# ScalarE's moves and exponentials in a hardware loop over heads, with one set of sum columns, in a one-core decode attention kernel

## The chip, the cores and the metric

The kernel runs on one core of a Trainium2 chip. The metric is the device time of one execution in microseconds (us).

## The reference

```python
# q: (1, 32, 1, 128), k and v: (1, 8, 65536, 128), all bf16
k = jnp.repeat(k, 4, axis=1)          # four query heads share one key/value head
v = jnp.repeat(v, 4, axis=1)
scores = jnp.einsum("bhqd,bhkd->bhqk", q, k) * 128 ** -0.5
p = _softmax(scores, axis=-1)
return jnp.einsum("bhqk,bhkd->bhqd", p, v)
```

One new token attends to 65,536 keys. Each byte of K and V (268.4 MB) is read once and used for four query rows.

## The kernel before

Each of the eight heads is two blocks of 32,768 keys, so there are sixteen blocks. For a block, VectorE transposes K, PE multiplies it with the queries (scores), ScalarE moves the scores from PSUM (where PE writes them) to SBUF (where VectorE and ScalarE then read them), VectorE and GpSimd find the maximum, ScalarE takes exponentials and their sums, and PE multiplies the result with V ("PV"). SyncEngine issues the loads, and sixteen DMA engines carry them out. K has two buffers, V has one. PE's code was in a hardware loop already (its instructions stand in the program once, and a branch goes back to them); ScalarE's and VectorE's were written out for all sixteen blocks.

ScalarE, before (this is what the change folds):

```python
        def move(j, u):
            if u == 0 and j >= 1:
                ac.wait_ge(ex_s, R * j)
            ac.wait_ge(qk_s, (j * U + u + 1) * GU)
            # ... cut: views fr (PSUM) and to (SBUF)
            for x in range(A):
                for a in range(A):
                    ins = ac.activation(to[...], fr[...], AF.Copy)      # 16 per call
            ins.then_inc(mv_s, 1)

        def exponent(i):
            h, b = divmod(i, C)
            ac.wait_ge(hma_s, i + 1)
            ac.activation(negb[b], ..., AF.Copy, scale=-scale).then_inc(nb_s, 1)
            if b:
                ac.wait_ge(df_s, h + 1)
                ac.activation(wgt, dif, AF.Exp, scale=scale).then_inc(wg_s, 1)
            # ... cut: waits for nb_s, mv_s
            if i >= 1:
                ac.wait_ge(pv_s, 2 * i)
            for g_ in range(R):
                ac.activation(pv[:, g_, :], sv[:, g_, :], AF.Exp, ...,
                              accum_out=rsum[h % 2][b][:, g_:g_ + 1]).then_inc(ex_s, 1)

        for j in range(N):              # N = 16, unrolled
            for u in range(U):          # U = 4
                move(j, u)
            exponent(j)
```

VectorE's end of a block, before. `weigh` rescales the first block of a head once the second one's maximum is known:

```python
        def collect(i):
            h, b = divmod(i, C)
            dv.wait_ge(pv_s, (i + 1) * 2)      # PV of block i is done
            if b == 0:
                dv.tensor_copy(o1, acc[:, 0:R]).then_inc(co_s, 1)
                return
            weigh(h)                           # three small operations
            # ... cut: add, wait for the sums' all-reduce (ls_s), reciprocal, multiply
```

The loads, whose order fixes what each DMA engine does: K of block j, then V of block j-1, each 8.4 MB as 128 rows. The last blocks are cut into pieces.

```python
        def load_k(i):
            if i >= NK:
                sp.wait_ge(tr_s, (i - NK + 1) * G)      # block i-2 is transposed
            # ... cut: the loads
        def load_v(i):
            if i < N - HALVED:
                if i >= 1:
                    sp.wait_ge(pv_s, 2 * i)             # PV of block i-1 is done
                # ... cut: the load, and the last blocks in pieces
```

## Time and profile before

| | before |
|---|---|
| device time, first three runs | 635.66 us median (635.41 to 635.75) |
| span of the profiled execution | 634.3 us |
| mean data rate over the span | 424 GB/s |
| busiest compute engine | VectorE, 54% |
| 8 KB instruction fetches in the span | 14 |

The page of the kernel before. The first lines are the busy time of each engine with its share of the span and its number of instructions, then the busy tenths of the DMA engines in forty slices, then the DMA queues with packets, MB, and share of sixteen engines' time:

```profile
span 634.3 us, 18751 instructions
...
PE 269.9 (43%) x8194; PEld 243.9 (38%) x8194; DVE 341.1 (54%) x411; ACT 275.7 (43%) x1178; POOL 10.5 (2%) x32
...
DMA  9999999999999999999999999999999999999995
...
DMA packets 6824, 268.68 MB, mean 424 GB/s; under 512 B 1045, under 2 KB 1045, under 8 KB 1685
...
q1 hardware_dynamic: 6612, 268.45, 98.4%
q8 instruction: 5, 0.08, 0.1%
q14 instruction: 15, 0.11, 0.0%
```

Data fill the DMA engines almost from the first slice to the last, and no compute engine passes 54%. So the kernel is limited by how fast the engines move 268 MB. The lines for q8 and q14, the queues of the instruction fetches (packets that the page labels "instruction"; e3 and e6 show that an engine's added code brings more of them), look like nothing: 0.19 MB of instructions, 0.1% of the time of sixteen engines. The share is an average over sixteen engines. If a fetch delays only one of them, 0.1% of sixteen is 1.6% of one. And at the end of this kernel a load was complete only with its slowest engine: in the tail below, PE's product at 629.67 us had still waited for V, though fifteen of the sixteen engines had moved all their data by 627.67 us.

The longest waits that matter here (engine, line, what it waited for: us in total, times, longest):

```profile
DVE ktb L276 <- DMA kbuf<-in_k_dram: 158.4, 17, 12.0
...
ACT pts L383 <- PE acc L196: 34.9, 15, 8.8
POOL small L154 <- DVE small L309: 30.8, 8, 12.2
...
DVE small L305 <- PE acc L196: 18.2, 7, 2.7
...
DVE small L322 <- POOL small L154: 3.4, 7, 0.5
```

VectorE waits for K from memory. ScalarE's exponentials wait for PV; the bias and weight that they need are ready earlier. This is the timeline of ScalarE near the end of block 7 (start us, duration us, engine, line, operation, idle before it):

```profile
302.61 0.21 ACT L372 ACTIVATE small<-small 128x4 f32<-128x4 f32 x1 [1.37 <-POOL small L162]
...
302.81 0.20 ACT L375 ACTIVATE small<-small 128x4 f32<-128x4 f32 x1
304.65 0.33 SPq L115 DMA_DIRECT2D vbuf<-in_v_dram  x1
...
304.74 0.86 ACT L383 ACTIVATE pts<-scs,small 128x256 bf16<-128x256 f32 x1 [1.73 <-PE acc L196]
```

Bias and weight are finished at 303.01 us, PV releases the exponentials at 304.74. ScalarE has about 1.7 us of slack there.

The tail of the timeline, PE's last PV products and the output store:

```profile
626.09 1.85 PE L196 MATMUL acc<-pts,vbuf 128*128 128x4 bf16 x64 [1.46 <-DMA vbuf<-in_v_dram]
...
628.47 1.01 PE L196 MATMUL acc<-pts,vbuf 128*128 128x4 bf16 x32 [0.54 <-DMA vbuf<-in_v_dram]
...
629.67 0.59 PE L196 MATMUL acc<-pts,vbuf 128*128 128x4 bf16 x16 [0.19 <-DMA vbuf<-in_v_dram]
...
630.77 0.57 PE L196 MATMUL acc<-pts,vbuf 128*128 128x4 bf16 x16
...
631.88 0.68 SPq L147 DMA_DIRECT2D out_dram<-oTX  x1
```

The first three of these groups of products each wait for a piece of V.

**Packets, engine by engine.** The page does not show single DMA engines, but the trace keeps start, duration, size and queue of every packet. Between 100 and 600 us sixteen packets are under way in 494 of the 500 us, and each starts within about 10 ns of the end of another. So packets can be chained by abutting times into sixteen chains, which I take for the sixteen engines. Two chains that end at the same nanosecond can swap names; the sorted times below hardly depend on that. From the kernel before, the start of the first 16 KB packet on each chain (the last K block) and the end of the last value packet:

```
                        earliest   9th     15th    16th (last)   us from the span's start
start of last K block    563.91   564.92  567.42   570.34
end of the data          626.17   626.82  627.67   630.46
```

One engine, called the straggler from here on, is about 2.9 us behind all others. The fetches on queue 14, 8 KB each, start at 34.5, 75.7, 95.6, 171.3, 222.7, 243.6, 291.1, 366.8, 425.6, 428.4, 489.1, 562.4, 597.8 and 618.8 us (the page counts 15 packets because of one 40-byte packet at the start). This is what one of them does to the data on its engine:

```
start us   took ns   bytes    queue
361.993     2422     65536    data
364.412     2422     65536    data
366.831      309      8192    q14 instruction
367.136     2798     65536    data
369.931     2419     65536    data
```

The next packet starts 0.302 us late and itself takes 0.376 us longer than the usual 2.422, so the engine loses 0.68 us to a fetch of 0.31 us. The data packets behind the nine ScalarE fetches from 34.5 to 562.4 us take 2.789 to 2.801 us. Followed through the chains, the nine ScalarE fetches from 34.5 to 562.4 us lie on the straggler: nine times 0.68 is 6.1 of the 6.4 us by which it starts the last K block after the earliest engine. VectorE's four fetches (75.7, 243.6, 428.4 and 597.8 us) cost more: the 64 KB packets after the first three take 3.080 us each, so the loss at 243.6 us is 0.97 us.

### The profile page before, as it was taken

Reading aid. Unit: us, or ns where it says so; the run is one execution under the profiler, and the core shown is the slowest. Engines: PE = TensorE matmul, PEld = TensorE weight load, DVE = VectorE, ACT = ScalarE, POOL = GpSimd, SP = SyncE. Lnnn points to the kernel's source line nnn. Section 1 sums busy time; section 2 is a strip of 40 time slices with the busy share of each in tenths; the row PEclk is TensorE's granted clock in tenths of the full one; section 3 lists DMA queues with packets and bytes.
Section 4 is the critical chain, followed back from the end, with each engine's and each line's share of the span. In section 5 each row is a group of like instructions: output and inputs, shape, how many; then the busy total and the mean of one; then the engine's idle time right before and its main releaser. Section 6 shows DMA issues by size and latency. Waiting matters only on the chain.

```text
span 634.3 us, 18751 instructions
## 1 busy us (share of the span) xinstructions
PE 269.9 (43%) x8194; PEld 243.9 (38%) x8194; DVE 341.1 (54%) x411; ACT 275.7 (43%) x1178; POOL 10.5 (2%) x32
## 2 busy tenths in 40 slices
PE   1314536144361534526255261553614437146525
PEld 1214436144361433525245261442614436146424
DVE  4649166390853809447193571926619176295710
ACT  0456425164351734617255261542616425165720
POOL 0000000000000000000000000000000000000000
DMA  9999999999999999999999999999999999999995
GB/s 365 433 446 426 434 426 439 438 422 446 422 442 434 430 426 434 446 413 451 422 446 426 434 430 430 446 414 455 413 450 422 438 426 438 438 401 437 431 349 222
DMA packets 6824, 268.68 MB, mean 424 GB/s; under 512 B 1045, under 2 KB 1045, under 8 KB 1685
## 3 DMA queue, kind: packets, MB, share of 16 engines
q1 hardware_dynamic: 6612, 268.45, 98.4%
q8 instruction: 5, 0.08, 0.1%
q14 instruction: 15, 0.11, 0.0%
q10 hardware_dynamic: 192, 0.03, 0.0%
HBM read 268.47 MB, written 0.01 MB: 423 GB/s over the span
## 4 chain that ended last, share of the span: by engine, by line
DMA 48%; DVE 27%; PE 14%; another core or an unknown queue 9%; SPq 1%; issue 1%; POOL 0%; DVEq 0%
DMA kbuf<-in_k_dram 30%; DVE ktb L276 25%; DMA vbuf<-in_v_dram 17%; PE acc L196 13%; PE qkb L185 1%; DVE small L283 1%; SPq L115 1%; POOL small L154 0%; PE acc L244 0%; DVE small L322 0%; DVE small L309 0%; DVE small L305 0%; DVE oTX L348 0%; DVE oTX L346 0%
## 5 line engine op out<-in xcount | busy, mean ns | idle before, releaser
L276 DVE STREAM_TRANSPOSE ktb<-kbuf 128x1024 int32<-128x1024 int32 x256 | 295.9, 1215 | 161.3 <-DMA kbuf<-in_k_dram 158.4
L366 ACT ACTIVATE scs<-qkb 32x64 f32<-32x64 f32 x1024 | 220.4, 215 | 281.5 <-PE qkb L185 270.3
L185 PE MATMUL qkb<-qblk,ktb 128*128 x4096 | 157.0, 176 | 343.4 <-DVE ktb L276 330.5
L185 PEld LDWEIGHTS qkb<-qblk,ktb 128*128 128x128 bf16 x4096 | 132.6, 105 | 367.5 <-issue 199.5
L196 PE MATMUL acc<-pts,vbuf 128*128 128x4 bf16 x4096 | 112.5, 166 | 17.9 <-DMA vbuf<-in_v_dram 17.4
L196 PEld LDWEIGHTS acc<-pts,vbuf 128*128 128x128 bf16 x4096 | 111.1, 104 | 19.6 <-DMA vbuf<-in_v_dram 15.8
L283 DVE TENSOR_REDUCE small<-scs 128x4 f32<-128x256 f32 x64 | 37.9, 593 | 61.4 <-ACT scs L366 61.4
L383 ACT ACTIVATE pts<-scs,small 128x256 bf16<-128x256 f32 x64 | 48.9, 853 | 34.9 <-PE acc L196 34.9
L162 POOL PARTITION_ALL_REDUCE small<-small x16 | 5.9, 370 | 575.0 <-DVE small L294 575.0
L383 ACT ACTIVATION_READ_ACCUMULATOR pts<-scs,small 128x1 f32 x64 | 13.7, 214 | 0.0
L316 DVE COPY small<-acc 128x4 f32<-128x4 f32 x8 | 1.3, 162 | 22.3 <-PE acc L196 22.3
L372 ACT ACTIVATE small<-small 128x4 f32<-128x4 f32 x16 | 3.3, 205 | 21.7 <-POOL small L162 21.7
L305 DVE TENSOR_TENSOR small<-small 128x4 f32<-128x4 f32 x8 | 1.3, 163 | 18.3 <-PE acc L196 18.2
L346 DVE TENSOR_TENSOR oTX<-acc,small 128x4 bf16<-128x4 f32 x1 | 0.2, 163 | 13.7 <-PE acc L196 13.7
L154 POOL PARTITION_ALL_REDUCE small<-small x8 | 3.4, 430 | 30.8 <-DVE small L309 30.8
L299 DVE TENSOR_TENSOR small<-small 128x4 f32<-128x4 f32 x8 | 1.3, 163 | 4.0 <-POOL small L162 4.0
L294 DVE TENSOR_REDUCE small<-small 128x4 f32<-128x16 f32 (+1 forms) x16 | 2.9, 184 | 0.5
L322 DVE RECIPROCAL small<-small 128x4 f32<-128x4 f32 x7 | 1.2, 178 | 3.4 <-POOL small L154 3.4
L307 DVE TENSOR_TENSOR small<-small 128x4 f32<-128x4 f32 x8 | 1.3, 157 | 2.7 <-ACT pts L383 2.7
L356 ACT ACT_TABLE_LOAD x1 | 1.3, 1283 | 2.7 <-issue 2.7
L375 ACT ACTIVATE small<-small 128x4 f32<-128x4 f32 x8 | 1.6, 205 | 0.0
L309 DVE TENSOR_TENSOR small<-small 128x4 f32<-128x4 f32 x8 | 1.3, 163 | 0.3
(19 smaller groups left out, 7.2 us busy)
## 6 DMA issues: line engine op xcount, KB each, us to landing
vbuf<-in_v_dram SPq DMA_DIRECT2D x3, 4096.0 KB, 25.5
kbuf<-in_k_dram SPq DMA_DIRECT2D x5, 2048.0 KB, 40.6
kbuf<-in_k_dram SPq DMA_DIRECT2D x1, 4096.0 KB, 22.3
vbuf<-in_v_dram SPq DMA_DIRECT2D x1, 2048.0 KB, 12.5
kbuf<-in_k_dram SPq DMA_DIRECT2D x2, 512.0 KB, 4.7
kbuf<-in_k_dram SPq DMA_DIRECT2D x1, 1024.0 KB, 7.3
vbuf<-in_v_dram SPq DMA_DIRECT2D x1, 1024.0 KB, 14.6
vbuf<-in_v_dram SPq DMA_DIRECT2D x1, 512.0 KB, 15.3
```

The costliest lines, as they stand in the source:

```text
L115: sp.dma_start(buf[:, a * D:b * D], src(t, i)[:, a * D:b * D]).then_inc(s, 16)
L154: g.partition_all_reduce(lsum, rhead, P, bass.bass_isa.ReduceOp.add).then_inc(ls_s, 1)
L162: g.partition_all_reduce(mtot if b else mfirst, hmax[:, b * R:(b + 1) * R], P, bass.bass_isa.ReduceOp.max,).then_inc(hma_s, 1)
L185: ins = pe.matmul(qkb[g // GU][:, at:at + A * R], lhsT=kt[:, be // NE, be % NE, n * P:(n + 1) * P], rhs=qblk[:, bass.ds(qcols[be], A * R)] ...
L196: ins = pe.matmul(acc[:, 0:R], lhsT=vbuf[:, t * D:(t + 1) * D], rhs=pts[:, t * R:(t + 1) * R], start=t == 0, stop=t == T - 1,)
L276: dv.transpose(to.rearrange("p (b t j) -> p b t j", b=NB, t=TG), fr.rearrange("p (t b i) -> p b t i", b=NB, t=TG),).then_inc(tr_s, 1)
L283: dv.tensor_reduce(hp[j % C][:, u * R:(u + 1) * R], scs[:, u * W:(u + 1) * W].rearrange("p (n g) -> p g n", g=R), AX.X, ALU.max,).then_inc ...
L294: dv.tensor_reduce(hmax[:, b * R:(b + 1) * R], hp[b].rearrange("p (u g) -> p g u", g=R), AX.X, ALU.max,).then_inc(hm_s, 1)
L366: ins = ac.activation(to[a * S4:(a + 1) * S4, x, :, :], fr[x * S4:(x + 1) * S4, a, :, :], AF.Copy)
L372: ac.activation(negb[b], mtot if b else mfirst, AF.Copy, scale=-scale).then_inc(nb_s, 1)
L375: ac.activation(wgt, dif, AF.Exp, scale=scale).then_inc(wg_s, 1)
L383: ac.activation(pv[:, g_, :], sv[:, g_, :], AF.Exp, bias=negb[b][:, g_:g_ + 1], scale=scale, accum_out=rsum[h % 2][b][:, g_:g_ + 1],).then ...
```

## The change

Its intent: run ScalarE's moves and exponentials in a hardware loop with one turn per head, two blocks a turn. This loop's body names the same buffers in each turn, so the two alternating sets of sum columns become one; so that they are free in time, VectorE's weighting moves ahead of the wait for PV, and ScalarE waits for it (`rh_s`) before it overwrites the sums.

```diff
-    rsum = [[cols(R) for _ in range(C)] for _ in range(2)]
+    rsum = [cols(R) for _ in range(C)]
 ... (VectorE: rsum[h % 2][b] becomes rsum[b])
             if b == 0:
                 dv.tensor_copy(o1, acc[:, 0:R]).then_inc(co_s, 1)
                 return
-            weigh(h)
 ...
             block_maximum(j)
+            if j >= C and j % C == 0:
+                weigh(j // C - 1)
             if j >= 1:
                 collect(j - 1)
 ... (ScalarE)
-        for j in range(N):
-            for u in range(U):
-                move(j, u)
-            exponent(j)
+        with nc.Fori(0, H, 1, engines=bass.OrderedEngineSet([ac.engine]), head_slot={ac.engine: 0}) as h:
+            for b in range(C):
+                ac.wait_ge(ex_s, h * (C * R) + b * R)
+                for u in range(U):
+                    ac.wait_ge(qk_s, h * (C * G) + (b * U + u + 1) * GU)
+                    move(b, u)
+                ac.wait_ge(hma_s, h * C + (b + 1))
+                ac.activation(negb[b], mtot if b else mfirst, AF.Copy, scale=-scale).then_inc(nb_s, 1)
+                if b:
+                    ac.wait_ge(df_s, h + 1)
+                    ac.activation(wgt, dif, AF.Exp, scale=scale).then_inc(wg_s, 1)
+                else:
+                    ac.wait_ge(rh_s, h)
 ... (waits for nb_s, mv_s, pv_s and the four exponentials as before, with h in the sums)
```

## The prediction

> **What bounds the kernel now.** The data transfers. The page gives 268.68 MB at a mean of 424 GB/s in a 634.3 us span, and the data queue's packets take 98.4% of sixteen engines' time. No compute engine passes 54%. By the groups view ScalarE waits for PE's scores before moves (270.3 us) and for PV before exponentials (34.9 us). In the timeline its bias and weight are done at 303.0 us, PV at 304.6: 1.6 us of slack, then 14 us idle before the next moves.
>
> **The sixteen DMA engines do not finish together.** By the trace's packet records the last value packets end at 626.2 to 627.7 us on fifteen engines and at 630.46 on one, and the tail waits for that one. At the last K block (first 16 KB packets) one engine starts at 570.34 us, the next latest at 567.42, the earliest at 563.92: it is 2.9 us behind the second-worst, 6.4 behind the best, and never idle at the tail, where others pause 1 to 2.5 us.
>
> **Why that one.** Beside the data, the trace has instruction fetches: queue 8, five of 16 KB, all before 48 us (PE's loop); queue 14, fourteen of 8 KB from 34.5 us on. Ten of these, about 65 us apart, fit ScalarE's unrolled code (76 instructions a block, 128 a fetch); four, about 170 us apart, fit VectorE. Tracked by abutting packets, the ScalarE fetches fall mostly on one engine; each delays a 64 KB packet by 0.30 us and stretches it from 2.42 to 2.79: 0.67 us. Ten make 6.7 us, which fits the straggler.
>
> **What the change removes.** It folds about 1220 ScalarE instructions into a body of about 200 (152 for moves and exponentials, four small, waits, register work)[...]. The arithmetic and the bytes of K and V stay. The ten fetches should become one to three early ones, 5 us or more off the straggler. The second-worst engine then sets the end, so only 2.9 us of it count (2.3 to 3.6).
>
> **What it adds and moves.** Register arithmetic and a branch on ScalarE, [...]inside the 1.6 us slack and the 14 us idle. VectorE's three weighting operations (0.16 us each) move ahead of the wait for PV, so the sums' all-reduce (0.43 us) leaves the time after PV on odd blocks; but VectorE's next transposes wait some 11 us for K: nothing gained. The new wait for the sums is met before PV ends.
>
> **The risk.** [...]This trace's PE loop[...]: seventeen turns[...], no fetch on queue 8 after 48 us. If ScalarE's loop refetches two or three pages a turn, 16 to 24 fetches replace ten, and it is 4 to 9 us slower.
>
> **Predicted:** 633.0 us, range 631.0 to 636.2. Faster by over 2%: 1%; within 2%: 97%; slower by over 2%: 2%.
>
> **What would show it.** Right: queue 14's packets fall from 15 to about 6, the last value packets on all engines end within about 1.5 us, mean GB/s rises by about 2, VectorE's wait for the sums (3.4 us) vanishes. Wrong: queue 14 has 20 packets or more; or the fetches go and one engine still lags by 3 us (then PE's fetches or something else made the straggler); or ScalarE becomes the releaser of exponentials in place of PV.

No term of the sum is cut: 635.7 us less the 2.9 us of the straggler's lead that count is 632.8, recorded as 633.0. The 128 instructions a fetch fit the traces and runs: ScalarE's fetches in the kernel before are about 66 us apart and a block takes 38.7 us, so a fetch lasts 1.7 blocks of 76 instructions, about 130; later 1280 added GpSimd instructions brought ten fetches and 640 brought five (e6, e8). A page in the risk is what one fetch brings; two or three of them a turn were the assumption. What remains of the risk's argument is PE's loop: in the kernel before its five fetches on queue 8 start from 14.4 to 47.0 us, and none follows.

## The result, and the profile after

The kernel after took 632.74 us (median; 632.66 to 632.87, four runs), beside 635.70 us (635.41 to 636.16) for the kernel before. The ratio is 0.9953, with a 95% interval of 0.9936 to 0.997. A ratio here and below is the mean time of one kernel's fast runs over the mean of the other's of the same rounds, so it is not quite the ratio of the medians. The gain of 3.0 us is clear of the noise, and far below the 2% that would be called faster.

The page of the kernel after, the lines that answer to those of before:

```profile
span 630.9 us, 18889 instructions
...
PE 270.0 (43%) x8194; PEld 244.0 (39%) x8194; DVE 340.4 (54%) x411; ACT 275.6 (44%) x1178; POOL 10.4 (2%) x32
...
DMA  9999999999999999999999999999999999999995
...
DMA packets 6816, 268.62 MB, mean 426 GB/s; under 512 B 1044, under 2 KB 1044, under 8 KB 1684
...
q1 hardware_dynamic: 6612, 268.45, 98.8%
q8 instruction: 5, 0.08, 0.1%
...
q14 instruction: 7, 0.06, 0.0%
```

The engines do the same work: ScalarE has 1178 instructions in both, 275.7 and 275.6 us busy. What fell is queue 14: fifteen packets to seven, 0.11 to 0.06 MB. Three of the seven are ScalarE's (at 7.0, 11.5 and 62.5 us), the other four VectorE's. The rate is up from 424 to 426 GB/s.

The same waits (line numbers have shifted):

```profile
DVE ktb L276 <- DMA kbuf<-in_k_dram: 162.2, 17, 11.5
...
ACT pts L387 <- PE acc L196: 34.2, 15, 9.8
...
DVE small L319 <- PE acc L196: 15.5, 7, 2.2
POOL small L154 <- DVE small L309: 13.2, 1, 13.2
```

ScalarE's exponentials wait for PV as long as before. The weighting no longer stands behind PV: what follows PV on odd blocks is now the addition (L319), and the 3.4 us that VectorE waited for the sums' all-reduce are gone from the head-by-head work. VectorE then waits longer for K (158.4 to 162.2 us): the time that the change gave VectorE was only waited out.

ScalarE at the end of block 7:

```profile
302.63 0.21 ACT L375 ACTIVATE small<-small 128x4 f32<-128x4 f32 x1 [1.36 <-POOL small L162]
...
302.83 0.21 ACT L378 ACTIVATE small<-small 128x4 f32<-128x4 f32 x1
304.67 0.33 SPq L115 DMA_DIRECT2D vbuf<-in_v_dram  x1
...
304.68 0.86 ACT L387 ACTIVATE pts<-scs,small 128x256 bf16<-128x256 f32 x1 [1.64 <-PE acc L196]
```

Bias and weight end at 303.04 us, 0.03 us later than before, and PV still releases the exponentials. The loop's register work does not show on this path.

The tail:

```profile
622.56 1.84 PE L196 MATMUL acc<-pts,vbuf 128*128 128x4 bf16 x64 [1.44 <-DMA vbuf<-in_v_dram]
...
624.98 1.01 PE L196 MATMUL acc<-pts,vbuf 128*128 128x4 bf16 x32 [0.57 <-DMA vbuf<-in_v_dram]
...
626.19 0.59 PE L196 MATMUL acc<-pts,vbuf 128*128 128x4 bf16 x16 [0.20 <-DMA vbuf<-in_v_dram]
...
627.34 0.57 PE L196 MATMUL acc<-pts,vbuf 128*128 128x4 bf16 x16
...
628.45 0.67 SPq L147 DMA_DIRECT2D out_dram<-oTX  x1
```

The product over the last piece but two (the first group of 16) starts at 626.19 us, before at 629.67: 3.5 us earlier. That is more than the 3.0 us between the medians, because the profiled execution of the kernel before was a slow one for it (636.09 us against a median of 635.70). The engines, by the packet records:

```
                        earliest   9th     15th    16th (last)   us from the span's start
start of last K block    564.02   564.76  567.20   567.48
end of the data          623.67   624.23  626.21   627.04
```

The earliest nine engines reach the last K block when they did before. The engine that was alone at 570.34 us has gone; the last is now at 567.48, which is 2.86 us earlier and about where the second-worst stood.

### The profile page after: what moved, and what is told of

Its sections match the earlier page's. It is cut to its first block, busy times and chain, and to the rows that moved or that the text cites. A ratio compares the mean times of both kernels' runs of the same rounds, so it can differ in the third digit from the quotient of the medians.

```text
span 630.9 us, 18889 instructions
## 1 busy us (share of the span) xinstructions
PE 270.0 (43%) x8194; PEld 244.0 (39%) x8194; DVE 340.4 (54%) x411; ACT 275.6 (44%) x1178; POOL 10.4 (2%) x32
## 4 chain that ended last, share of the span: by engine, by line
DMA 66%; DVE 22%; PE 10%; SPq 1%; issue 1%; DVEq 0%
DMA kbuf<-in_k_dram 59%; DVE ktb L276 21%; PE acc L196 8%; DMA vbuf<-in_v_dram 7%; PE qkb L185 2%; DVE small L283 1%; SPq L115 1%; PE acc L244 0%; DVE oTX L349 0%; DVE oTX L347 0%; DVEq L346 0%
## 5 line engine op out<-in xcount | busy, mean ns | idle before, releaser
L276 DVE STREAM_TRANSPOSE ktb<-kbuf 128x1024 int32<-128x1024 int32 x256 | 295.9, 1212 | 165.1 <-DMA kbuf<-in_k_dram 162.2
L319 DVE TENSOR_TENSOR small<-acc,small 128x4 f32<-128x4 f32 x7 | 1.1, 162 | 15.5 <-PE acc L196 15.5
```

The source lines that it names most:

```text
L276: dv.transpose(to.rearrange("p (b t j) -> p b t j", b=NB, t=TG), fr.rearrange("p (t b i) -> p b t i", b=NB, t=TG),).then_inc(tr_s, 1)
```

## The experiments

Theory A: each of ScalarE's instruction fetches delays one DMA engine by about 0.67 us; ScalarE's written-out code put ten of them on one engine; a load waits for its slowest engine; the loop took seven of the ten away, and the end moved up to the next-worst engine. Rivals: B, the gain is the weighting that left VectorE's time after PV, or the single set of sums; C, fetches do no harm and something else held that engine back; D, the number of executed ScalarE instructions matters, not their fetching; E, only ScalarE's code matters because it is on the softmax path.

All outputs are right. "Fetches" are 8 KB packets on queue 14 in the span; VectorE's four are in each count unless noted.

| run | what it is | us, median (range) | before, same rounds | ratio (95%) | fetches |
|---|---|---|---|---|---|
| e1_unrolled | after, loop written out | 635.67 (635.45 to 636.20) | 635.89 | 0.9999 (0.9985 to 1.0013) | 14 |
| e2_pairs | before, loop over two heads | 632.83 (632.54 to 632.93) | 635.89 | 0.9953 (0.9939 to 0.9966) | 8 |
| e3_pad_unrolled | before, +1216 ScalarE instructions | 642.25 (642.13 to 642.26) | 635.89 | 1.01 (1.0085 to 1.0116) | 23 |
| e4_pad_loop | after, the same 1216 in the loop | 632.85 (632.78 to 632.89) | 635.89 | 0.9953 (0.994 to 0.9967) | 8 |
| e5_quads | before, loop over four heads | 638.80 (638.75 to 638.93) | 635.48 | 1.0052 (1.0038 to 1.0066) | 18 |
| e6_pad_pool | after, +1280 GpSimd instructions | 635.95 (635.59 to 636.04) | 635.48 | 1.0005 (0.9991 to 1.0018) | 17 |
| e7_dve_loop | after, VectorE looped too | 631.46 (631.36 to 632.03) | 635.48 | 0.9938 (0.9924 to 0.9951) | 6 |
| e8_pad_pool_half | after, +640 GpSimd instructions | 632.52 (632.50 to 632.75) | 635.61 | 0.9954 (0.994 to 0.9967) | 12 |
| e9_after_again | after | 632.86 (632.66 to 632.98) | 635.61 | 0.9958 (0.9944 to 0.9971) | 7 |
| e10_dve_loop_again | as e7 | 632.10 (631.62 to 632.34) | 635.61 | 0.9945 (0.9931 to 0.9958) | 6 |

### The two parts apart: e1 and e2

e1 keeps all of the change but the loop:

```diff
-        with nc.Fori(0, H, 1, ...) as h:
+        for h in range(H):
```

> The kernel after with ScalarE's hardware loop written out again; one set of sum columns, the new wait and the moved weighting stay. Theory A (instruction fetches delay one DMA engine): fourteen 8 KB fetches after 30 us come back, one engine lags the next by about 3 us again, 635.7 us (635.0 to 636.4). Rival B (the gain comes from the weighting leaving VectorE's time after PV, or from the single set of sums): 632.7 us.

Measured: 635.67 us, ratio 0.9999. The moved weighting, the new wait and the single set of sums are worth nothing. The last engine starts the last K block at 570.20 us, the next one at 567.43: the straggler is back, with the fetches (the page's line for queue 14):

```profile
q14 instruction: 14, 0.11, 0.0%
```

e2 is the other half: the kernel before with a loop over pairs of heads, so that the two sets of sums can stay and the weighting stays behind PV.

```diff
-        for j in range(N):
-            for u in range(U):
-                move(j, u)
-            exponent(j)
+        with nc.Fori(0, H // 2, 1, ...) as t:
+            for i in range(4):
+                hh, b = divmod(i, C)
+                ... moves and exponentials, sums to rsum[hh % 2][b]
```

> The kernel before with only the loop: ScalarE loops over pairs of heads, two sets of sums, weighting in its old place. Body about 340 instructions[...]. Theory A: ScalarE's ten fetches become three or four, 632.7 us (632.3 to 633.5). Rival B: 635.7 us. If the body did not stay[...], three or so fetches in each of the four turns would give 635.7 or more.

Measured: 632.83 us, ratio 0.9953, the ratio of the whole change. Its line for queue 14:

```profile
q14 instruction: 8, 0.07, 0.0%
```

Eight fetches, four of them ScalarE's. The loop alone is the gain; rival B has fallen.

### Is it the fetch or the execution: e3 and e4

e3 adds to the kernel before 152 waits after each block's exponentials, on a semaphore that has long had its value. They compile to 76 instructions a block. e4 puts the same lines into the loop of the kernel after.

```diff
+                for _ in range(152):
+                    ac.wait_ge(init_s, 2)
```

> The kernel before with 152 waits a block that are always met (76 instructions) added after ScalarE's exponentials, unrolled: about 1216 instructions, 9 to 10 more 8 KB fetches. Theory A: 9.5 x 0.67 us more on the engine that already is last, 642.0 us (640.0 to 643.5). Rival C (fetches do not delay the data; something else made that engine last): 635.7 us, whether or not the fetches are there.

> The kernel after with the same 152 met waits a block inside its hardware loop: body about 330 instructions. The same instructions are executed as in the padded unrolled one, without their fetches. Theory A: 632.7 us (632.4 to 633.5), at most five ScalarE fetches. Rival D (ScalarE's executed instructions cost the time, not their fetching): as much slower than after as the padded unrolled one is than before.

Measured: e3 642.25 us, 6.4 us above before; e4 632.85 us, 0.1 us from what the kernel after measures (632.74 and 632.86). These are the pages' instruction counts and queue lines, e3 first:

```profile
span 640.4 us, 19968 instructions
...
q14 instruction: 23, 0.19, 0.1%
```

```profile
span 631.0 us, 20105 instructions
...
q14 instruction: 8, 0.07, 0.0%
```

Both execute about 1217 instructions more than their parents (19968 against 18751, and 20105 against 18889, the pages' totals). In the written-out form they bring nine more fetches, in the loop one. Nine fetches for 6.36 us is 0.71 us a fetch, close to the 0.67 read from the packets. Rivals C and D have fallen: instructions that do nothing, on an engine that is 43% busy, slowed the kernel by 1% (6.36 us) with nine more fetches, and by no more than 0.1 us with one. In e3 the last engine starts the last K block at 575.91 us, 8.3 us behind the next.

### How long may a loop body be: e5

The loop of e2 over four heads a turn: about 660 instructions, two turns.

> The loop alone again, over four heads a turn: body about 660 instructions[...], two turns. If a loop body of that size stays[...], five or six ScalarE fetches in all and 632.7 to 633.8 us. If it does not[...], the second turn fetches its pages again, ten or eleven in all, and theory A gives 635.7 us as for the unrolled code.

Measured: 638.80 us, 3.3 us slower than before, and worse than both expectations. Queue 14 again:

```profile
q14 instruction: 18, 0.15, 0.1%
```

Of 18 fetches 14 are ScalarE's, at 6.9, 11.5, 62.4, 118.7, 184.7, 250.7, 307.0, 310.1, 315.6, 374.4, 433.1, 496.7, 565.1 and 610.8 us. The second turn begins in the cluster at 307 to 316 us, and from there the code is fetched again. In the chains, the fetches from 62.4 to 496.7 us all lie on one chain, and that chain ends last, at 633.29 us against 629.22 for the next. So the body of about 660 instructions was fetched again in its second turn, while the one of about 340 was not (e2: no ScalarE fetch after 118.6 us). ScalarE itself shows no wait for these fetches: the only idle time for which its list of waits names no releaser is 2.7 us at the start, in e5 as in the kernel before. The direction was expected. The count was not: I had reckoned with ten or eleven, because I left out the extra fetches at the jump back. By the rate of 0.7 us a fetch, four more than before are 2.8 us; measured 3.3. (What is cut out of the expectations of e2 and e5 are sizes in KB, a limit among them, and where the code is kept, which no run shows. That a body "stays" means here that it is not fetched again.)

### Does it matter whose code it is: e6 and e8

e6 gives the padding to GpSimd, which is 2% busy and hardly on the path: in the kernel after, 160 met waits a block, written out (80 instructions). e8 has half of them.

```diff
         for n in range(N):
             b = n % C
+            for _ in range(160):          # e8: 80
+                g.wait_ge(init_s, 2)
             g.wait_ge(hm_s, n + 1)
```

> The kernel after with 160 waits a block that are always met (80 instructions, 1280 in all) unrolled on GpSimd, which is 2 per cent busy. Theory A: ten more 8 KB fetches, on whichever DMA engine serves GpSimd; 6.7 us on an engine that is not among the late ones, of which 3.3 us are slack behind the engine that is last in after: 636 us (635 to 639.5 if it is one of the late ones). Rival E (only ScalarE's code matters, since it shares the softmax path): 632.7 us.

> The kernel after with half the padding on GpSimd: 80 met waits a block, 40 instructions, 640 in all, five more fetches. Theory A with slack: 5 x 0.67 us = 3.4 us on GpSimd's DMA engine is about the slack that this engine has behind the one that is last in after, so 632.7 to 633.3 us. If each fetch cost the same whether or not its engine is last, half of what the full padding cost: 634.3 us.

Measured: e6 635.95 us, 3.1 to 3.2 us above the kernel after, which did not run in the same rounds (the kernel before did: 635.48 us); e8 632.52 us, not above the 632.86 of e9, which ran beside it. Queue 14, e6 and then e8:

```profile
q14 instruction: 17, 0.14, 0.1%
```

```profile
q14 instruction: 12, 0.10, 0.0%
```

Ten added fetches for an idle engine gave back the whole gain of the change, so rival E has fallen. Five added fetches cost nothing. In e6 one engine is again alone at the last K block (570.95 us, the next 567.46); in e8 the last two are at 567.46 and 567.38. So the cost had a threshold in these two runs: the fetches counted only from where their engine became the last one. GpSimd's cost about as much as ScalarE's: in e8 the packet after the one at 153.6 us takes 2.771 us, a loss of 0.65 us.

### A version that beats both: e7, e9, e10

VectorE's code still had four fetches. e7 loops it over heads 1 to 6 (its first and last heads differ and stay written out), in the kernel after:

```diff
+        head(0, first=True)
+        with nc.Fori(1, H - 1, 1, engines=bass.OrderedEngineSet([dv.engine]), head_slot={dv.engine: 0}) as h:
+            head(h)
+        head(H - 1, last=True)
```

> The kernel after with VectorE's code too in a hardware loop (heads 1 to 6; head 0 and head 7 stay written out): its instructions fall from about 470 to 250. Theory A: VectorE's four 8 KB fetches (about 0.97 us each) become one or two, and the engine that carried them is no longer last; the next one is 0.8 us earlier by the last packets of after: 631.9 us (631.2 to 632.5). If the register work of its waits slows VectorE's chain of transposes: above 632.7 us.

Measured: 631.46 us. The kernel after had not run in those rounds, so both were run together:

> The kernel after, unchanged, on the same chip and in the same rounds as the one with VectorE looped, to compare the two directly: 632.7 us.

> The kernel after with VectorE's code looped too, repeated beside after: 631.5 us, 1.2 us below after. If the first result was a difference between chips: no difference to after.

Measured: 632.10 us (631.62 to 632.34) beside 632.86 (632.66 to 632.98). The ranges of five runs do not overlap, and the difference is 0.76 us, less than the 1.3 of the comparison across rounds (631.46 beside 632.74). It is a small gain; the intervals of the two ratios to before overlap, so I call it about 1 us and not more. Queue 14 in e10:

```profile
q14 instruction: 6, 0.05, 0.0%
```

VectorE still has three fetches (at 73.2, 79.0 and 576.5 us), where I had expected one or two. The last engine starts the last K block at 567.35 us, in e9 at 567.50, so that time hardly moves. What moves is the end of the data: 625.99 us, in e9 627.13. By the chains, the engine of VectorE's fetches starts the last K block at 566.15 us in e10 and at 567.15 in e9. That is 1.0 us earlier, about what one of its fetches costs. In both runs it meets one more fetch after that. That it was the engine that ended last in e9 fits, but ties between chains near the end leave it unproven.

## Why the prediction was right

1. *Limit.* The kernel is bound by its data; the engines' busy times are the same to 1 us before and after, and e4 shows that 1216 more executed ScalarE instructions cost nothing. Shown.
2. *One late DMA engine.* Predicted 2.9 us behind the next. The change moved the latest start of the last K block from 570.34 to 567.48 us, that is 2.86 us, and the median device time by 3.0. Shown, by e1 (late engine back, time back) and e2 (gone, gain there).
3. *Fetches are its cause, 0.67 us each.* e3 measured 0.71 a fetch over nine. e6 made an engine late by adding fetches for GpSimd alone. Shown.
4. *Only part of the removed delay counts.* Seven fetches less at 0.67 us are 4.7 us on that engine; 3.0 arrived, because another engine was next. e8 shows the same threshold from the other side: five added fetches, no time.
5. *The loop's own costs are hidden.* Bias and weight 0.03 us later on the block looked at, PV still the releaser. ScalarE's new wait for VectorE (`rh_s`) never shows in the list of waits, as predicted. Shown for this body.
6. *The weighting moved early is worth nothing.* e1, ratio 0.9999. The wait for the sums vanished as predicted, and VectorE waited for K instead.
7. *The risk of refetching.* It did not arise in the change but is real: e5's longer body met it and was slower than the unrolled code.

Wrong was one sign that I named: "the last value packets on all engines end within about 1.5 us". They end over 3.4 us (623.67 to 627.04), one of them still 0.8 us behind the next. I had taken the narrow spread of the fifteen engines before (626.17 to 627.67) for the natural one. It was made by the straggler: fast engines had run out of issued loads at the tail, paused, most by 1 to 2.5 us, and so drew level. With the straggler gone the longest such pause is about 0.9 us, and their own lateness shows.

What stays open: seven engines of the kernel after reach the last K block late, by about 1.5 to 3.5 us. There are five 16 KB fetches for PE early on, on queue 8 and by the chains on different engines, and one engine each for VectorE's and ScalarE's, which would make seven; seven are late in e10 too (565.67 to 567.35 us, the next at 564.92). That fits, but no run took PE's fetches away. Why a fetch also stretches the data packet beside it is open too.

## What to carry to other kernels

In a kernel that is bound by its loads, look at the slowest DMA engine and not at the mean: here an instruction stream that is 0.1% of the DMA time held one of sixteen engines 2.9 us behind the next, and the end of the kernel with it. Written-out code cost time here even on an idle engine, once its fetches made their DMA engine the last one (e6, ten fetches, 3.1 us), and below that it cost nothing (e8, five). A hardware loop took them away here only where its body was not fetched again, so check the fetch count in the profile: ScalarE's body of some 340 instructions was not, and the one of 660 was and lost 3.3 us against no loop at all. Where between them the limit lies was not measured.
